# Windowed attention in front of two expert layers: scores issued one unit earlier on four PSUM banks, and half of the probability copies on ScalarE

## The chip, the cores and the metric

One core of a Trainium2 chip runs the whole program. The metric is the device time of one execution in microseconds (us); lower is better. Three timed runs of the kernel before took 779.24, 786.21 and 785.84 us, so the median is 785.84 us. One more execution was taken with the hardware profiler, and every row below is from that one.

## What is computed

```python
def reference(**kwargs):
    ...
    attn_out = _attn_ref(**attn_kwargs)          # B=4, H=8, 512 local + 32 global tokens, head size 64
    x = attn_out.transpose(0, 2, 1, 3).reshape(B * S, H * D)   # 2176 x 512
    x = _moe_ref(x=x, **moe_kwargs)              # top-1 of 8 experts, 512 -> 1024 -> 512, ReLU
    return _moe2_ref(x=x, **moe2_kwargs)         # 512 -> 2048 -> 512 with a piecewise square
```

The attention is the part that the change touches. A local query sees the 32 global keys and the local keys at most 32 positions away; a global query sees all 544 keys. Both go through a softmax over their keys.

```python
    s_g = scale * np.matmul(q_g, k_all.transpose(0, 1, 3, 2))
    out_g = np.matmul(sm(s_g), v_all)
    mask = np.abs(pos[:, None] - pos[None, :]) <= 32
    s_ll = np.where(mask, scale * np.matmul(q_l, k_l.transpose(0, 1, 3, 2)), -1e9)
    s_l = np.concatenate([scale * np.matmul(q_l, k_g.transpose(0, 1, 3, 2)), s_ll], axis=-1)
    out_l = np.matmul(sm(s_l), np.concatenate([v_g, v_l], axis=2))
```

## The kernel before

The attention works on the 32 (batch, head) pairs in order. Heads 2c and 2c+1 form a *pair* c: their queries and keys share one SBUF tile (64 partitions each), and there are 16 pairs. The work is cut into *units*: 32 units "h" (one local head each) and 8 units "g" (the global queries of four heads). The list `units` (L538 to L544) has a g unit ahead of every four h units, with two exceptions (the first and the last g unit).

The parts that one head goes through are separate functions, and the loop at L577 calls them in different units, so that each part finds its input ready:

- `s_pair(c)` (L209): for both heads of a pair, one matmul each with a mask matrix (L213) opens a PSUM bank and adds 0 or -1e30, then 32 small matmuls (L218) add the scores. It runs in the even unit, the one of head 2c.
- `s_max(n)` (L221): VectorE takes the row maxima out of PSUM (L225) and negates them (L226). Then it does up to 8 small operations of a list `fill` (routing of earlier tokens to experts).
- `s_exp(n)` (L232): ScalarE takes the exponentials, four instructions of 128x128 with a running sum (L239).
- `t_head(n)` (L287), two units later: TensorE transposes the four 128x128 blocks into a PSUM bank (L294), VectorE copies the bank to the SBUF tile `pto` (L295).
- `pv(c)` (L328), one unit after the second head's `t_head`: 64 small matmuls with the values (L339), then VectorE multiplies by the reciprocal sum (L342 to L344) into `xr`.
- `x_turn(b, g)` (L351), one unit later through the list `tasks`: TensorE transposes `xr`, ScalarE copies the result to `xT` (L355). After four pairs (one batch) `logits`, `logits_t` and the list of `route` follow.
- The g units do the same with `s_glob` (L242), `g_max`, `g_exp` (L267), `t_glob` (L299, six transposes into two banks, copied by ScalarE at L306), `pv_glob` (L310).

The order of the instructions on each of TensorE, VectorE, ScalarE and the SyncE DMA queue is exactly the order in which the code issues them (the schedule is manual for these four), and each engine works through its own list in order. What an instruction waits for is set by the tiles. PSUM has 8 banks: before, 3 for the tag "s" (the scores of two heads and of a global unit share them), 3 for the tag "to" (every transpose target), one for "x" (the output of `pv`), and one, `gxb`, for small things. A new tile of a tag takes a bank whose last user has to be done.

The loads of keys, queries and values are issued by SyncE (`load_k`, `load_q`, `load_v`) into 4, 3 and 3 buffers, in the odd units after the tasks, or behind `pv`. GpSimd spreads the values (`spread_v`). After the attention come the tail of the routing, the expert layer and the last layer (from about 155 us on), which the change doesn't touch except for line numbers.

Of the kernel before, what the change touches and what calls it, by code (L numbers as in the profile page):

```python
# [35 lines left out]
NB = 24  # L36
# [75 lines left out]
def emit(tc, d, out):  # L112
# [51 lines left out]
    nc.vector.memset(warm, 0.0)  # L164
    wps = ps.tile([128, 512], F32, tag="s", name="sp", bufs=3)
    for _ in range(9):
# [42 lines left out]
    def s_pair(c):  # L209
        k, q = ks[c], qp[c]  # L210
        for z in range(2):
            sps[2 * c + z] = ps.tile([128, 4, BW], F32, tag="s", name="sp", bufs=3)
            nc.tensor.matmul(sps[2 * c + z].rearrange("p i w -> p (i w)"), lhsT=mask[:, 0:128], rhs=mask[:, 128:], start=True, stop=False)  # L213
        for j in range(NG):
            i, a = divmod(j, 4)
            for z in range(2):
                r = slice(64 * z, 64 * z + 64)
                nc.tensor.matmul(sps[2 * c + z][a * WIN:(a + 1) * WIN, i, :], lhsT=q[r, j * WIN:(j + 1) * WIN],  # L218
                                 rhs=k_at(k, r, j), start=False, stop=(i == 3))
# [22 lines left out]
    def s_glob(q):  # L242
        sp = ps.tile([128, 512], F32, tag="s", name="sp", bufs=3)
        for part in range(3):
            for j in range(4):
                c, z = 2 * q + j // 2, 64 * (j % 2)
                k = ks[c][z:z + 64].rearrange("p (n w) -> p n w", w=WIN)
                p = slice(j * SG, (j + 1) * SG)
                o, r = ((sp[p, 0:320], ks[c][z:z + 64, 0:320]),
                        (sp[p, 320:480], k[:, 15:24:2, :]), (gxb[p, 0:64], k[:, 10:13:2, :]))[part]  # L250
                nc.tensor.matmul(o, lhsT=qg[z:z + 64, c, :], rhs=r, start=True, stop=True)
        gsp[q] = sp
# [34 lines left out]
    def t_head(n):  # L287
        c, z = divmod(n, 2)
        if z == 0:
            pt[c] = ap.tile([128, 2, 512], F32, tag="pto", name="pto", bufs=3)  # L290
        p = pexp.pop(n)
        o = ps.tile([128, 4, 128], F32, tag="to", name="ps_o", bufs=3)
        for i in range(4):
            nc.tensor.transpose(o[:, i, :], p[:, i, :], ident)  # L294
        nc.vector.tensor_copy(pt[c][:, z, :], o.rearrange("p i q -> p (i q)"))  # L295

    pgt, grec = {}, {}

    def t_glob(q):  # L299
        pg = gexp.pop(q)  # L300
        pgt[q] = ap.tile([128, 6, 128], F32, tag="pgt", name="pgt", bufs=2)
        for m0, m1 in ((0, 4), (4, 6)):
            o = ps.tile([128, 4, 128], F32, tag="to", name="ps_o", bufs=3)
            for m in range(m0, m1):
                nc.tensor.transpose(o[:, m - m0, :], pg[:, m * 128:(m + 1) * 128], ident)
            nc.scalar.activation(pgt[q][:, m0:m1, :], o[:, 0:m1 - m0, :], AF.Copy)  # L306
# [21 lines left out]
    def pv(c):  # L328
        b, g = divmod(c, 4)
        p, v = pt.pop(c), vt[c]  # L330
        if g == 0:
            xr[b] = ap.tile([128, 4, DM], F32, tag="xr", name="xr", bufs=2)
            xT[b] = ap.tile([128, 4, SL], F32, tag="xT", name="xT", bufs=2)
        xo = ps.tile([128, 4, 2, D], F32, tag="s" if c == 15 else "x", name="xo", bufs=3 if c == 15 else 1)
        for i in range(4):
# [15 lines left out]
    def x_turn(b, c):  # L351
        o = ps.tile([128, 4, 128], F32, tag="to", name="ps_x", bufs=3)
        for i in range(4):
# [4 lines left out]
    def logits(b):  # L358
        o = ps.tile([128, 512], F32, tag="to", name="lg", bufs=3)
        for c in range(4):  # L360
# [6 lines left out]
    def logits_t(b):  # L367
        o = ps.tile([128, 4, 4, 32], F32, tag="to", name="lg", bufs=3)
        for i in range(4):
# [3 lines left out]
    def logits3():  # L373
        o = ps.tile([128, 512], F32, tag="to", name="lg", bufs=3)
        for c in range(3):
# [5 lines left out]
    def part3():  # L381
        o = ps.tile([128, 4, 4, 32], F32, tag="to", name="lg", bufs=3)
        for i in range(4):
# [11 lines left out]
    def glob_turn():  # L395
        o = ps.tile([128, 4, 128], F32, tag="to", name="ps_x", bufs=3)
        for c in range(4):
# [96 lines left out]
    def zlist():  # L494
        o = ps.tile([128, 512], F32, tag="to", name="ip", bufs=3)[:, 0:1]
        for t in range(NE):
# [8 lines left out]
    def zsteps():  # L505
        o = ps.tile([128, 4, 128], F32, tag="to", name="ps_x", bufs=3)
        for k in range(4):
# [3 lines left out]
        for g in range(2):  # L511
            o = ps.tile([128, 4, 128], F32, tag="s", name="zh", bufs=3)
            for u in range(4):
# [58 lines left out]
    for c in range(3):  # L572
        spread_v(c)
    pend_n, pend_g, pend_v = [], [], []
    LT, LG = 2, 3
    nv = 3
    for s in range(len(units)):  # L577
# [5 lines left out]
        if gq[0] == "g":  # L583
            t_glob(gq[1])
            pend_g.append(gq[1])
        if kind == "h":
            if a % 2 == 0:
                s_pair(a // 2)
        elif kind == "g":
            s_glob(a)  # L590
        while tasks:
            if tasks.pop(0)() == 1:
                break
        if kind == "h" and a % 2 == 1:
            if a // 2 + 4 < 16:
# [122 lines left out]
    zz(24)  # L718
    ip = ps.tile([128, 512], F32, tag="to", name="ip", bufs=3)[:, 0:NB]
    for t in range(NT):  # L720
# [525 lines left out]
```

## Time and profile before

| | |
|---|---|
| timed runs | 779.24, 786.21, 785.84 us, median 785.84 us |
| the profiled execution's own time | 777.55 us |
| its span, first to last instruction | 775.8 us |
| share of the span: TensorE, VectorE, ScalarE busy | 96%, 67%, 46% |
| mean granted TensorE clock | 0.991 |

The profiled execution took 777.55 us with 1.75 us outside its span, and lies 8.29 us under the median of the timed runs. Times in the rows are in us from the start of the span. A timeline row gives start, duration, engine, line, operation, output and inputs, shapes and a count, and in brackets how long the engine was idle before it and who released it. "PE" is TensorE's matmul side and "PEld" its weight loads; DVE is VectorE, ACT ScalarE, POOL GpSimd, SPq SyncE's queue of DMA issues. Consecutive instructions of one kind are merged into one row, so a row that took long for its count has waits inside.

### The profile page before, as it was taken

The numbers are of one execution on the slowest core, as the hardware profiler recorded it, in microseconds if no ns is written. First come the engines' busy times: TensorE is split into PE (matmuls) and PEld (weight loads), VectorE is DVE, ScalarE is ACT, GpSimd is POOL, SyncE is SP. The second block draws the span as 40 slices with busy tenths as digits, with TensorE's granted clock in tenths as the row PEclk, the third lists the DMA queues.
The fourth block names the chain that finished last, engine by engine and source line by source line (L and its number), as shares of the span: only waits on it lengthen the run. The fifth ranks groups of instructions, "written<-read, shape, count | busy, mean of one in ns | idle before, by whom it ended". The sixth has DMA issues, their size and how long they took to land.

```text
span 775.8 us, 16281 instructions
## 1 busy us (share of the span) xinstructions
PE 742.9 (96%) x6525; PEld 645.5 (83%) x6539; DVE 520.8 (67%) x988; ACT 360.6 (46%) x775; POOL 123.9 (16%) x164
## 2 busy tenths in 40 slices
PE   7898868899999999999999999999999999999996
PEld 3666646699899899899899989999898999999994
DVE  3687856758956956957477767767875787555443
ACT  3667545355755855854345554323432442322221
POOL 2536423231122122111100000000000000002112
PEclk9999999999999999999999999999999999999999
DMA  8868872188968956912142221110220100001111
GB/s 259 260 195 254 269 236 76 39 295 316 347 201 274 351 197 242 361 47 82 61 124 82 71 93 54 55 55 1 66 88 11 55 1 0 1 1 68 54 41 68
DMA packets 41954, 103.77 MB, mean 134 GB/s; under 512 B 6798, under 2 KB 11278, under 8 KB 39824
## 3 DMA queue, kind: packets, MB, share of 16 engines
q1 hardware_dynamic: 37312, 88.48, 34.3%
q0 software_dynamic: 4560, 14.19, 4.9%
q8 instruction: 53, 0.87, 0.5%
q14 instruction: 29, 0.24, 0.1%
HBM read 93.45 MB, written 14.18 MB: 139 GB/s over the span
## 4 chain that ended last, share of the span: by engine, by line
PE 72%; issue 6%; POOL 1%; DVE 1%; ACT 0%; POOLq 0%
PE fh L919 7%; PE fh L920 7%; PE fh L921 7%; PE o L920 7%; PE o L921 7%; PE o L919 7%; PE hp L919 5%; PE hp L921 5%; PE hp L920 5%; PE yp L921 5%; PE yp L919 4%; PE yp L920 4%; PE xTp L902 1%; POOL out_dram L1160 1%; PE yTp L813 1%
## 5 line engine op out<-in xcount | busy, mean ns | idle before, releaser
L1107 DVE SCALAR_TENSOR_TENSOR r<-r 128x384 f32<-128x384 f32 (+1 forms) x96 | 51.4, 535 | 120.0 <-ACT r L1106 119.8
L1106 ACT ACTIVATE r<-fh,half 128x384 f32<-128x384 f32 (+1 forms) x96 | 54.0, 563 | 115.1 <-PE fh L921 114.9
L921 PE MATMUL o<-wh,gl 128*128 128x512 f32 x272 | 107.5, 395 | 0.0
L919 PE MATMUL o<-wh,gh 128*128 128x512 f32 x272 | 107.4, 395 | 0.0
L920 PE MATMUL o<-wl,gh 128*128 128x512 f32 x272 | 107.3, 394 | 0.0
L1109 ACT ACTIVATE gh<-g 128x384 fp32r<-128x384 f32 (+1 forms) x96 | 48.8, 508 | 125.5 <-DVE g L1108 125.5
L920 PE MATMUL fh<-yl,wh 128*128 128x384 f32 (+1 forms) x320 | 104.4, 326 | 0.0
L919 PE MATMUL fh<-yh,wh 128*128 128x384 f32 (+1 forms) x320 | 104.3, 326 | 0.0
L921 PE MATMUL fh<-yh,wl 128*128 128x384 f32 (+1 forms) x320 | 104.2, 326 | 0.0
L1160 POOL DMA_INDIRECT out_dram<-acc,rid x17 | 16.5, 969 | 368.3 <-DVE acc L1158 366.8
L919 PE MATMUL hp<-xTh,w1h 128*128 128x256 f32 x256 | 72.5, 283 | 1.8 <-PEq L1051 1.8
L921 PE MATMUL hp<-xTh,w1l 128*128 128x256 f32 x256 | 72.5, 283 | 0.0
L920 PE MATMUL hp<-xTl,w1h 128*128 128x256 f32 x256 | 72.5, 283 | 0.0
L920 PEld LDWEIGHTS fh<-yl,wh 128*128 128x128 f32 x320 | 60.1, 188 | 3.6 <-DVE rid L817 0.2
L919 PEld LDWEIGHTS fh<-yh,wh 128*128 128x128 f32 x320 | 60.1, 188 | 3.5
L921 PEld LDWEIGHTS o<-wh,gl 128*128 128x128 f32 x272 | 51.1, 188 | 12.4 <-DVE gl L1115 0.8
L919 PE MATMUL yp<-w2h,hTh 128*128 128x512 f32 x152 | 60.4, 398 | 0.0
L921 PEld LDWEIGHTS fh<-yh,wl 128*128 128x128 f32 x320 | 60.1, 188 | 0.0
L921 PE MATMUL yp<-w2h,hTl 128*128 128x512 f32 x152 | 59.6, 392 | 0.0
L920 PE MATMUL yp<-w2l,hTh 128*128 128x512 f32 x152 | 59.3, 390 | 0.0
L920 PEld LDWEIGHTS o<-wl,gh 128*128 128x128 f32 x272 | 51.1, 188 | 7.9
L919 PEld LDWEIGHTS o<-wh,gh 128*128 128x128 f32 x272 | 51.1, 188 | 7.8
(232 smaller groups left out, 1573.8 us busy)
## 6 DMA issues: line engine op xcount, KB each, us to landing
w1r<-in_w SPq DMA_DIRECT2D x44, 512.0 KB, 5.7
w2r<-in_w SPq DMA_DIRECT2D x44, 512.0 KB, 5.3
wraw<-in_wf SPq DMA_DIRECT2D x16, 1024.0 KB, 4.9
ks<-in_k SPq DMA_DIRECT2D x16, 400.0 KB, 5.5
v<-in_v SPq DMA_DIRECT2D x16, 384.0 KB, 3.8
yr<-ys SPq DMA_DIRECT2D x17, 256.5 KB, 2.7
qp<-in_q SPq DMA_DIRECT2D x16, 256.0 KB, 6.5
xs<-xr SPq DMA_DIRECT2D x8, 512.0 KB
```

The lines of the kernel that those rows point to most:

```text
L813: nc.tensor.transpose(p[:, k, :], a[:, k * 128:(k + 1) * 128], ident)
L902: nc.tensor.transpose(p[:, k, :], src[:, k * 128:(k + 1) * 128], ident)
L919: nc.tensor.matmul(o, lhsT=ah, rhs=bh, start=first, stop=False)
L920: nc.tensor.matmul(o, lhsT=ah, rhs=bl, start=False, stop=False)
L921: nc.tensor.matmul(o, lhsT=al, rhs=bh, start=False, stop=last)
L1106: nc.scalar.activation(r[:, 0:w], o[:, 0:w], AF.Relu, bias=half, scale=0.5)
L1107: nc.vector.scalar_tensor_tensor(r[:, 0:w], r[:, 0:w], 1.0, r[:, 0:w], ALU.min, ALU.mult)
L1109: nc.scalar.activation(gh[:, 0:w], g[:, 0:w], AF.Copy)
L1160: w = nc.gpsimd.indirect_dma_start(out=out, out_offset=bass.IndirectOffsetOnAxis(ap=rid[:, tt:tt + 1].bitcast(U32), axis=0), in_=a, in_off ...
```

## The change

PSUM: the tag "s" gets 4 banks, the tag "to" 2. `s_pair(0)` is issued ahead of the loop. In the loop `s_pair(c + 1)` is issued in the odd unit of pair c, after the tasks and ahead of the loads, instead of `s_pair(c)` in the even unit of its own pair. `t_head` of every odd head has its bank copied by ScalarE instead of VectorE.

```diff
-        o = ps.tile([128, 4, 128], F32, tag="to", name="ps_o", bufs=3)
+        o = ps.tile([128, 4, 128], F32, tag="to", name="ps_o", bufs=2)
         for i in range(4):
             nc.tensor.transpose(o[:, i, :], p[:, i, :], ident)
-        nc.vector.tensor_copy(pt[c][:, z, :], o.rearrange("p i q -> p (i q)"))
+        if z:
+            nc.scalar.activation(pt[c][:, z, :], o.rearrange("p i q -> p (i q)"), AF.Copy)
+        else:
+            nc.vector.tensor_copy(pt[c][:, z, :], o.rearrange("p i q -> p (i q)"))
...
+    s_pair(0)
     pend_n, pend_g, pend_v = [], [], []
...
-        if kind == "h":
-            if a % 2 == 0:
-                s_pair(a // 2)
-        elif kind == "g":
+        if kind == "g":
             s_glob(a)
         while tasks:
             if tasks.pop(0)() == 1:
                 break
+        if kind == "h" and a % 2 == 1 and a < 31:
+            s_pair(a // 2 + 1)
         if kind == "h" and a % 2 == 1:
             if a // 2 + 4 < 16:
                 load_k(a // 2 + 4)
```

Every other `bufs=3` of the tags "s" and "to" becomes 4 and 2 in the same way (`wps`, `s_pair`, `s_glob`, `t_glob`, the last `pv`, `x_turn`, `logits`, `zlist`, `zsteps` and the other users).

On TensorE, in the middle of the attention (the g unit of the 6th group of four heads, then its first three h units), this stands in the kernel before; L294 is `t_head`, L213 and L218 `s_pair`, L354 `x_turn`, L339 `pv`, L305 `t_glob`:

```order
L339 MATMUL xo<-v,pto 32x64 x32
L294 MATMUL ps_o<-ident,p 128x128 x4
L213 LDWEIGHTS mask
L213 MATMUL sp<-mask 128x512
L213 LDWEIGHTS mask
L213 MATMUL sp<-mask 128x512
L218 MATMUL sp<-ks,qp 32x128 x32
L354 MATMUL ps_x<-ident,xr 128x128 x4
L339 MATMUL xo<-v,pto 32x64 x32
L294 MATMUL ps_o<-ident,p 128x128 x4
L305 MATMUL ps_o<-ident,pgz_121 128x128 x6
```

and this in the changed kernel, whose line numbers are 3 higher from `pv_glob`, `pv` and `x_turn` on (L342 is `pv`, L357 `x_turn`, L308 `t_glob`):

```order
L342 MATMUL xo<-v,pto 32x64 x32
L294 MATMUL ps_o<-ident,p 128x128 x4
L357 MATMUL ps_x<-ident,xr 128x128 x4
L213 LDWEIGHTS mask
L213 MATMUL sp<-mask 128x512
L213 LDWEIGHTS mask
L213 MATMUL sp<-mask 128x512
L218 MATMUL sp<-ks,qp 32x128 x32
L342 MATMUL xo<-v,pto 32x64 x32
L294 MATMUL ps_o<-ident,p 128x128 x4
L308 MATMUL ps_o<-ident,pgz_121 128x128 x6
```

The scores have moved behind `x_turn`, which now follows one `t_head` after the `pv` that feeds it, and they belong to the next pair. `t_glob` is followed by `x_turn` and not by scores.

On ScalarE, from the global exponentials (L275) of the next group on, before; L239 is `s_exp`, L355 the copy of `x_turn`, L306 those of `t_glob`:

```order
L275 ACTIVATE pgz_120,sg<-sp,m_2059 128x5x64
L275 ACTIVATE pgz_120,sg<-sp,m_2059 128x5x32
L275 ACTIVATE pgz_120,sg<-gxb,m_2059 128x2x32
L355 ACTIVATE xT<-ps_x 128x512
L239 ACTIVATE p,ss<-sp,mn 128x128 x8
L306 ACTIVATE pgt<-ps_o 128x512
L306 ACTIVATE pgt<-ps_o 128x256
```

and in the changed kernel, where L296 is the new copy of an odd head, L358 that of `x_turn`, L309 those of `t_glob`:

```order
L275 ACTIVATE pgz_120,sg<-sp,m_2095 128x5x64
L275 ACTIVATE pgz_120,sg<-sp,m_2095 128x5x32
L275 ACTIVATE pgz_120,sg<-gxb,m_2095 128x2x32
L296 ACTIVATE pto<-ps_o 128x512
L358 ACTIVATE xT<-ps_x 128x512
L239 ACTIVATE p,ss<-sp,mn 128x128 x8
L309 ACTIVATE pgt<-ps_o 128x512
```

A copy of an odd head now stands between the global exponentials and the copy of `x_turn`.

On VectorE, from the `t_head` of the first head of a group to the next g unit, before (L295 are the copies, L225 and L226 `s_max`, L318 the global output):

```order
L295 COPY pto_1555<-ps_o_1556 128x512
L225 TENSOR_REDUCE mx4_1616<-sp_1573 128x4
L226 TENSOR_SCALAR mn_1617<-mx4_1616 128x4
L295 COPY pto_1555<-ps_o_1625 128x512
L225 TENSOR_REDUCE mx4_1642<-sp_1575 128x4
L226 TENSOR_SCALAR mn_1643<-mx4_1642 128x4
L318 TENSOR_SCALAR xgo_1670<-gxb_119,rg_1488 128x64
L295 COPY pto_1682<-ps_o_1683 128x512
```

and in the changed kernel (L298 are the copies that stay, L321 the global output):

```order
L298 COPY pto_1591<-ps_o_1592 128x512
L225 TENSOR_REDUCE mx4_1616<-sp_1498 128x4
L226 TENSOR_SCALAR mn_1617<-mx4_1616 128x4
L225 TENSOR_REDUCE mx4_1678<-sp_1500 128x4
L226 TENSOR_SCALAR mn_1679<-mx4_1678 128x4
L321 TENSOR_SCALAR xgo_1706<-gxb_119,rg_1488 128x64
L298 COPY pto_1718<-ps_o_1719 128x512
```

The copy of the odd head is gone from the middle; the rest stands as before. SyncE's list of DMA issues is the same in both kernels.

## Rows read from the trace of the kernel before

**Rows 1.** Stretch, length, busy PE, PEld, DVE, ACT, POOL (count), PEclk, DMA share, GB/s

```profile
65.20:79.90 14.70, 13.73 (x373) 9.87 (x374) 10.39 (x26) 10.16 (x49) 8.08 (x17) 1.00 0.80 249
79.90:94.30 14.40, 12.52 (x365) 8.86 (x367) 12.74 (x41) 8.48 (x40) 6.08 (x8) 1.00 0.84 263
112.60:131.30 18.70, 13.73 (x362) 10.92 (x362) 15.09 (x54) 9.86 (x46) 9.22 (x15) 0.91 0.32 90
155.00:775.80 620.80, 612.03 (x3424) 551.97 (x3424) 416.07 (x670) 276.27 (x419) 62.02 (x54) 1.00 0.34 118
```

**Rows 2.** Timeline of TensorE, 69 to 92 us

```profile
69.45 1.38 PE L294 MATMUL ps_o<-ident,p 128*128 128x128 f32 x4
...
78.15 1.10 PE L339 MATMUL xo<-v,pto 128*32 128x64 f32 x64
79.18 0.66 PE L294 MATMUL ps_o<-ident,p 128*128 128x128 f32 x4
79.89 0.38 PE L213 MATMUL sp<-mask 128*128 128x512 bf16 x1
...
81.28 0.66 PE L354 MATMUL ps_x<-ident,xr 128*128 128x128 f32 x4
...
83.59 1.37 PE L294 MATMUL ps_o<-ident,p 128*128 128x128 f32 x4 [0.62 <-ACT p L239]
84.80 0.82 PE L305 MATMUL ps_o<-ident,pgz 128*128 128x128 f32 x6
...
88.42 0.66 PE L354 MATMUL ps_x<-ident,xr 128*128 128x128 f32 x4 [1.06 <-DVE pto L295]
...
90.25 1.24 PE L294 MATMUL ps_o<-ident,p 128*128 128x128 f32 x4
```

**Rows 3.** Timeline of TensorE: rows that resume inside a group

```profile
37.83 0.64 PE L218 MATMUL sp<-ks,qp 64*32 64x128 f32 x23 [1.76 <-issue]
...
67.42 0.41 PE L218 MATMUL sp<-ks,qp 64*32 64x128 f32 x3 [0.80 <-issue]
...
99.57 1.71 PE L339 MATMUL xo<-v,pto 128*32 128x64 f32 x52 [2.86 <-issue]
```

**Rows 4.** Timeline of ScalarE, 78 to 85 us

```profile
78.72 0.53 ACT L275 ACTIVATE pgz<-sp,m 128x320 f32<-128x320 f32 x1 [1.22 <-DVE ri L342]
...
81.98 0.60 ACT L355 ACTIVATE xT<-ps_x 128x512 f32<-128x512 f32 x1 [1.97 <-PE ps_x L354]
...
83.10 0.35 ACT L239 ACTIVATE p<-sp,mn 128x128 f32<-128x128 f32 x1
...
84.12 0.37 ACT L239 ACTIVATE p<-sp,mn 128x128 f32<-128x128 f32 x1
```

**Rows 5.** Timeline of VectorE, 79 to 88 us

```profile
79.32 0.69 DVE L344 TENSOR_TENSOR xr<-xo,ri 128x512 f32<-128x512 f32 x1 [0.38 <-PE xo L339]
...
81.39 0.69 DVE L225 TENSOR_REDUCE mx<-sp 128x4 f32<-128x512 f32 x1 [0.79 <-PE sp L218]
...
82.20 0.28 DVE L416 TENSOR_REDUCE L<-lg 128x32 f32<-128x128 f32 x1
...
85.15 0.20 DVE L281 TENSOR_SCALAR rg<-sg 128x1 f32<-128x1 f32 x1
...
87.68 0.68 DVE L295 COPY pto<-ps_o 128x512 f32<-128x512 f32 x1
```

**Rows 6.** Groups of instructions, 20 to 100 us: busy us, mean ns

```profile
L295 DVE COPY pto<-ps_o 128x512 f32<-128x512 f32 x21 | 14.4, 684 | 1.3 <-PE ps_o L294 1.1
...
L355 ACT ACTIVATE xT<-ps_x 128x512 f32<-128x512 f32 x11 | 6.6, 597 | 15.2 <-PE ps_x L354 15.2
```

**Rows 7.** Timeline near the start: a query load's issue and TensorE

```profile
19.25 0.35 SPq L179 DMA_DIRECT2D qp<-in_q  x1
...
22.46 0.38 PE L213 MATMUL sp<-mask 128*128 128x512 bf16 x1
```

**Rows 8.** DMA issues up to 30 us: KB each, us to landing

```profile
qp<-in_q SPq DMA_DIRECT2D x6, 256.0 KB, 7.6
```

**Rows 9.** The last stretch of the attention on TensorE

```profile
116.94 1.12 PE L354 MATMUL ps_x<-ident,xr 128*128 128x128 f32 x4 [2.85 <-DVE xr L344]
```

More of the change, by code (lines that the diff above doesn't have):

```diff
@@ L164, in emit @@
     nc.vector.memset(warm, 0.0)
-    wps = ps.tile([128, 512], F32, tag="s", name="sp", bufs=3)
+    wps = ps.tile([128, 512], F32, tag="s", name="sp", bufs=4)
     for _ in range(9):
@@ L211, in s_pair @@
         for z in range(2):
-            sps[2 * c + z] = ps.tile([128, 4, BW], F32, tag="s", name="sp", bufs=3)
+            sps[2 * c + z] = ps.tile([128, 4, BW], F32, tag="s", name="sp", bufs=4)
             nc.tensor.matmul(sps[2 * c + z].rearrange("p i w -> p (i w)"), lhsT=mask[:, 0:128], rhs=mask[:, 128:], start=True, stop=False)
@@ L242, in s_glob @@
     def s_glob(q):
-        sp = ps.tile([128, 512], F32, tag="s", name="sp", bufs=3)
+        sp = ps.tile([128, 512], F32, tag="s", name="sp", bufs=4)
         for part in range(3):
@@ L302, in t_glob @@
         for m0, m1 in ((0, 4), (4, 6)):
-            o = ps.tile([128, 4, 128], F32, tag="to", name="ps_o", bufs=3)
+            o = ps.tile([128, 4, 128], F32, tag="to", name="ps_o", bufs=2)
             for m in range(m0, m1):
@@ L333, in pv @@
             xT[b] = ap.tile([128, 4, SL], F32, tag="xT", name="xT", bufs=2)
-        xo = ps.tile([128, 4, 2, D], F32, tag="s" if c == 15 else "x", name="xo", bufs=3 if c == 15 else 1)
+        xo = ps.tile([128, 4, 2, D], F32, tag="s" if c == 15 else "x", name="xo", bufs=4 if c == 15 else 1)
         for i in range(4):
@@ L351, in x_turn @@
     def x_turn(b, c):
-        o = ps.tile([128, 4, 128], F32, tag="to", name="ps_x", bufs=3)
+        o = ps.tile([128, 4, 128], F32, tag="to", name="ps_x", bufs=2)
         for i in range(4):
@@ L358, in logits @@
     def logits(b):
-        o = ps.tile([128, 512], F32, tag="to", name="lg", bufs=3)
+        o = ps.tile([128, 512], F32, tag="to", name="lg", bufs=2)
         for c in range(4):
@@ L367, in logits_t @@
     def logits_t(b):
-        o = ps.tile([128, 4, 4, 32], F32, tag="to", name="lg", bufs=3)
+        o = ps.tile([128, 4, 4, 32], F32, tag="to", name="lg", bufs=2)
         for i in range(4):
@@ L373, in logits3 @@
     def logits3():
-        o = ps.tile([128, 512], F32, tag="to", name="lg", bufs=3)
+        o = ps.tile([128, 512], F32, tag="to", name="lg", bufs=2)
         for c in range(3):
@@ L381, in part3 @@
     def part3():
-        o = ps.tile([128, 4, 4, 32], F32, tag="to", name="lg", bufs=3)
+        o = ps.tile([128, 4, 4, 32], F32, tag="to", name="lg", bufs=2)
         for i in range(4):
@@ L395, in glob_turn @@
     def glob_turn():
-        o = ps.tile([128, 4, 128], F32, tag="to", name="ps_x", bufs=3)
+        o = ps.tile([128, 4, 128], F32, tag="to", name="ps_x", bufs=2)
         for c in range(4):
@@ L494, in zlist @@
     def zlist():
-        o = ps.tile([128, 512], F32, tag="to", name="ip", bufs=3)[:, 0:1]
+        o = ps.tile([128, 512], F32, tag="to", name="ip", bufs=2)[:, 0:1]
         for t in range(NE):
@@ L505, in zsteps @@
     def zsteps():
-        o = ps.tile([128, 4, 128], F32, tag="to", name="ps_x", bufs=3)
+        o = ps.tile([128, 4, 128], F32, tag="to", name="ps_x", bufs=2)
         for k in range(4):
@@ L511, in zsteps @@
         for g in range(2):
-            o = ps.tile([128, 4, 128], F32, tag="s", name="zh", bufs=3)
+            o = ps.tile([128, 4, 128], F32, tag="s", name="zh", bufs=4)
             for u in range(4):
@@ L718, in emit @@
     zz(24)
-    ip = ps.tile([128, 512], F32, tag="to", name="ip", bufs=3)[:, 0:NB]
+    ip = ps.tile([128, 512], F32, tag="to", name="ip", bufs=2)[:, 0:NB]
     for t in range(NT):
```

## The prediction

> **What bounds the kernel now.** I read the busy time by stretch first. From 155 us on TensorE is busy 612.03 of 620.80 us [rows 1], and the change touches nothing there, so it can only act on the attention, the first 131 us or so. One batch of the attention takes two stretches of about 14.5 us, one for each group of four heads. In the first shown TensorE is busy 13.73 of 14.70 us, in the second 12.52 of 14.40; VectorE 10.39 and 12.74, ScalarE 10.16 and 8.48 [rows 1]. No engine is full by itself, VectorE comes closest in the second stretch, and TensorE sets the pace as long as the others feed it.
>
> Then TensorE's timeline, for its stalls. Four transposes of a head take 0.66 us where nothing holds them (79.18), but 1.38, 1.37 and 1.24 us at 69.45, 83.59 and 90.25, where each waits for one of the four exponentials, and at 83.59 TensorE was idle 0.62 us before [rows 2]. That is the stall the change aims at: 0.72 us in the first stretch, and 0.62 + 0.71 + 0.58 = 1.91 us in the second. A fourth one, 1.06 us at 88.42, waits for VectorE's copy of an earlier head [rows 2]: together 2.97 us in the second stretch. The cause shows on ScalarE: it stood 1.97 us idle until the transposes of `x_turn` came at 81.98, and the exponentials behind them in its list began only at 83.10 [rows 4]; VectorE had waited 0.79 us for the scores at 81.39 [rows 5].
>
> A third kind of gap is no wait of the program: TensorE stopped in the middle of a group for 1.76, 0.80 and 2.86 us, with nothing that released it [rows 3]. I read it as late instruction supply. The Trainium skill ("Runtime: NRT & Kernel Launch", "Instruction fetch mechanics") says that crossing an instruction page is mostly hidden; these rows, 5.42 us in all, show it open. By the page the gaps would be nothing to reckon with; by the rows they are noise that the change doesn't aim at, and I leave them as they are.
>
> **The change part by part.** *Scores one unit earlier.* Nothing is added: the same matmuls, mask and scores, from 79.89 to 81.28, so 1.39 us a pair [rows 2], stand elsewhere. The maximum, and behind it the exponential, no longer waits for them, so the stalls at the head transposes should go: -0.72 in the first stretch, -1.91 in the second, and the 1.06 us goes too, since `x_turn` no longer waits on that copy, though the copy itself is as late as ever (next part). I credit 2.97 and 0.72. Four banks make it possible: the bank of the second head of `s_pair` in the first odd unit of a group was last used by the global scores, so it waits for the second of the global exponentials, not for the head just begun. These start at 78.72 [rows 4] and read that bank for about 0.9 us, to 79.6, before TensorE could be there: no wait.
>
> *What the scores had covered.* `x_turn` now comes one `t_head` after `pv`. VectorE's product `xr` began at 79.32, right after `pv` (78.15 + 1.10 = 79.25), and took 0.69, to 80.01 [rows 2, 5]; TensorE would want it at 79.18 + 0.6 = 79.8. In the second stretch the transposes of `x_turn` also share a bank with the `t_head` just ahead, as the other of the two is held by the routing's logits; that bank is emptied by ScalarE, behind the global exponentials, which end near 79.9, and a copy of 0.60 [rows 4, 6] puts it at 80.5. New stall: 0.5 us in the first stretch, 0.75 in the second.
>
> *Two banks for transposes.* The second part of `t_glob` takes the bank of the `t_head` ahead of it, and so waits for VectorE's copy. In the second stretch that copy ended at 87.68 + 0.68 = 88.36, which is 9.04 us after `xr` began [rows 5]. Taken off: the copy of the odd head, 0.6 of the 0.684 us of rows 6 (the rest overlapped), and the 0.79 us wait. That leaves 7.65. TensorE gets there from the end of `pv` in 0.6 (transposes) + 0.65 (stall of above, beyond the transposes) + 0.55 (`x_turn`) + 1.39 (scores) + 1.05 (`pv`) + 0.6 + 0.55 = 5.4. New stall: 2.2 us. In the first stretch the routing block on VectorE from 82.20 to 85.15 [rows 5], 2.95 us, is missing; 7.65 - 2.95 = 4.7 is earlier than 5.2, and only the copy's own 0.68 beside half a group of transposes shows: 0.2 us. The Trainium skill ("Perfetto Trace Analysis", "Matmuls") says that independent groups should rotate through different PSUM banks so that the emptying of one overlaps the matmuls of the next. It speaks against this part, and with three banks the same place (84.80) went through without a wait [rows 2]. By it the two banks cost what I reckon or more; that is the rival on the slow side below.
>
> *Odd heads copied by ScalarE.* 16 copies of 0.684 us leave VectorE, 16 of about 0.597 come to ScalarE [rows 6], two in each stretch. ScalarE was idle 4.5 and 5.9 us of a stretch [rows 1]; they hide there except where counted above. Behind such a copy in ScalarE's list stand the exponentials of the next head, 84.12 + 0.37 - 83.10 = 1.39 us [rows 4], which are used two units later.
>
> *Loads.* Queries are wanted one unit earlier. A load issued at 19.25 with 7.6 us to landing [rows 7, 8] is there at 26.9 at the latest; TensorE did `s_pair(2)` at 22.46 [rows 7], and would stand ahead of `s_pair(3)` at about that time now, with the scores of pair 2 already done. Bounds: a gain of 1.5 us (it lands at 23, and the early stalls go), a loss of 2 (it lands at 27, and everything behind waits). I take +0.3, near the middle. Later, a load is issued more than a stretch ahead.
>
> *The last batch.* From 112.60 on VectorE is busy 15.09 of 18.70 us [rows 1], and TensorE waited 2.85 us for its `xr` at 116.94 [rows 9]. Four copies fewer take 2.4 us off VectorE there; other waits stand in line, so between 0 and -2.4; I take -1.2.
>
> **The sum.** First stretch: -0.72 + 0.5 + 0.2 = 0.0. Second: -2.97 + 0.75 + 2.2 = 0.0. To these I add that VectorE, with 1.2 us less to do in a stretch, catches up a little: -0.3 us a batch, three batches, -0.9 (bounds -4 and +3, from 0 to all of what is counted as new stall being half or one and a half times as large). With +0.3 and -1.2 that is -1.8 us: 777.55 - 1.8 = 775.75 us for the profiled execution. The median of the runs lies 8.29 us higher, and against it the same difference gives 785.84 - 1.8 = 784.0 us.
>
> **Rivals.** *Slower: two banks are too few.* Place: the second part of `t_glob` and the `x_turn` transposes. If VectorE or ScalarE is further behind than in this trace (each waits for TensorE in its own list, and a stall of one is passed on), each of the new stalls grows. I count 3.65 us of them a batch; they would have to reach 3.65 + 1.8/3 = 4.25 to make the change worth nothing, and another 2.6 us a batch to cost over 1%. Twice as large in all three batches gives 784.0 + 11 = 795 us. For it: 2.2 us is from one row; against it: the scores come so early that VectorE no longer waits for them.
>
> *Faster: the new stalls don't come.* If VectorE, relieved of the odd copies and of its waits for scores, runs ahead of TensorE, the copy is done in time, and all old stalls are gained: 3.69 us a batch, three batches, and 2.4 at the end: -13 us, 773 us. For it: VectorE has 4.3 us idle in the first stretch; against it: 1.7 in the second [rows 1].
>
> *No effect: supply.* The DMA engines are busy 0.80 and 0.84 of the time in these stretches [rows 1], at 249 and 263 GB/s, and TensorE stood still without a releaser three times [rows 3]. What is gained waits for keys, values or instructions: 786 us, plus or minus 2.
>
> *It doesn't do what it says.* If the second bank of `s_pair` had been that of the head just begun, its scores would wait for that head's exponentials (78.72 + 1.2 + 1.2 + 1.39 = 82.5 instead of 80.5), 2 us a stretch, +13 us, 799. The program assigns it the bank of the global scores, so I give this 0.02.
>
> **How the numbers follow.** About 1%, 7.8 us, is what a measurement of this kernel can tell from no change. The forecast (784.0) has 0.50, supply 0.20, both within 1%; faster 0.20, of which 0.18 passes 1%; slower 0.10 with the misread bank, all over 1%. That is 0.18 faster, 0.72 within, 0.10 slower. The range has to take in the faster case, 773, and the lower half of the slower one: 772 to 792.
>
> **What would show it.** Right: transposes of a head at 0.66 us nearly everywhere, no idle time of VectorE before the maxima, a stall of TensorE before the second part of `t_glob` (about 2 us in every second stretch) and one of 0.5 to 0.75 before `x_turn`, stretches of 14 to 14.5 us. Wrong: stretches of 13 us or less (the faster rival), or over 15 (the slower one); a wait for scores at the mask matmul of the second head; a wait for a query load after the start.

## The result: 5.7 us slower, and the profile after

Sixteen runs of each kernel: 789.40 us median after, 784.27 us before (its first three had given 785.84). The ratio of the two is 1.0073, 95% interval 1.0045 to 1.0100, so the change costs 0.73% of 784.27, 5.7 us, where I had forecast a gain of 1.8. Three of the sixteen runs after stood in a slower state (793.67 to 794.38 us, granted clock 0.976 to 0.978); without them the means are 788.32 and 783.80 us, 4.5 us apart, so the loss is 4 to 6 us and what is reckoned from 1.0073 below can be about 1 us too large. The profiled execution of the changed kernel took 786.55 us, its span is 784.8 us (775.8 before), and its mean granted clock is 0.984 (0.991). These two executions differ by 9.00 us, more than the medians do: that of the kernel before lies 6.7 us below its median, that of the changed kernel 2.9 us. What follows reads the difference of the two profiles, so it is larger than the loss in the median.

I cut the attention at the global scores of a group (L251), which stand in both kernels, and at the last `ranks`. Busy time by stretch, before: one batch in two stretches, then from the 7th to the 8th group's global scores, then all that is left of the attention, which I call the last batch (columns as in [rows 1]).

```profile
61.65:76.51 14.86, 13.35 (x370) 9.36 (x371) 11.07 (x30) 9.90 (x46) 10.50 (x18) 1.00 0.89 272
76.51:91.41 14.90, 13.01 (x370) 9.37 (x371) 12.59 (x38) 8.75 (x41) 4.10 (x9) 1.00 0.79 246
91.41:107.61 16.20, 11.49 (x309) 8.90 (x311) 8.88 (x26) 7.42 (x34) 7.53 (x13) 0.89 1.01 332
107.61:138.43 30.82, 25.68 (x630) 20.20 (x632) 20.42 (x68) 15.92 (x67) 10.65 (x19) 0.94 0.29 84
```

The same four stretches after:

```profile
63.84:78.75 14.91, 12.87 (x370) 8.85 (x371) 8.35 (x23) 11.15 (x49) 9.09 (x16) 1.00 0.76 238
78.75:93.57 14.82, 12.15 (x370) 9.23 (x371) 11.24 (x41) 9.70 (x43) 6.09 (x12) 1.00 0.83 272
93.57:110.20 16.63, 10.06 (x244) 7.43 (x244) 7.16 (x20) 7.32 (x32) 6.11 (x11) 0.84 0.98 322
110.20:147.18 36.98, 28.78 (x629) 21.88 (x631) 17.78 (x64) 17.68 (x70) 10.64 (x19) 0.84 0.22 61
```

A batch takes as long as before (29.73 and 29.76 us), with TensorE less busy in it (25.02 against 26.36). The last batch is 6.16 us longer, and its granted clock has fallen from 0.94 to 0.84. TensorE's timeline in the second stretch answers [rows 2]:

```profile
81.42 0.66 PE L294 MATMUL ps_o<-ident,p 128*128 128x128 f32 x4
82.80 0.66 PE L357 MATMUL ps_x<-ident,xr 128*128 128x128 f32 x4 [0.72 <-ACT pto L296]
83.50 0.38 PE L213 MATMUL sp<-mask 128*128 128x512 bf16 x1
...
87.44 0.31 PE L342 MATMUL xo<-v,pto 128*32 128x64 f32 x6 [1.47 <-issue]
87.69 0.66 PE L294 MATMUL ps_o<-ident,p 128*128 128x128 f32 x4
...
89.16 0.44 PE L308 MATMUL ps_o<-ident,pgz 128*128 128x128 f32 x2 [0.38 <-DVE pto L298]
```

The head transposes take 0.66 us, the old stalls are gone, and `x_turn` waits 0.72 us for ScalarE's copy (forecast 0.75). But the second part of `t_glob` waits 0.38 us and not 2.2, and in front of it stands a gap that I hadn't reckoned with there: 1.47 us of "issue", that is, TensorE stood still and the profile shows nothing that it waited for. I call such gaps *stops*. More rows of that kind, which answer [rows 3]:

```profile
36.28 0.53 PE L342 MATMUL xo<-v,pto 128*32 128x64 f32 x20 [2.14 <-issue]
57.47 0.58 PE L342 MATMUL xo<-v,pto 128*32 128x64 f32 x25 [1.41 <-issue]
66.95 0.24 PE L342 MATMUL xo<-v,pto 128*32 128x64 f32 x1 [0.96 <-issue]
100.00 1.09 PE L218 MATMUL sp<-ks,qp 64*32 64x128 f32 x57 [1.59 <-issue]
106.93 1.11 PE L308 MATMUL ps_o<-ident,pgz 128*128 128x128 f32 x4 [4.00 <-issue]
```

With the 1.47 and one of 0.21 (at 71.26) that is 11.78 us from the third to the last group's global scores. Before it was the 5.42 us of [rows 3] and one more, which the profile puts down to VectorE (the instruction named had ended at 105.84, 0.75 us earlier, so I count it as a stop):

```profile
106.59 0.66 PE L354 MATMUL ps_x<-ident,xr 128*128 128x128 f32 x4 [1.75 <-DVE mn L226]
```

together 7.17 us. The growth doesn't hang on this one pair of executions: in the profiles of `p_copy` and `before_warm` below, which have the same TensorE list there as the kernel before, these stops sum to 7.8 and 7.3 us, in those of `p_score` and `after_warm`, with the list of the changed kernel, to 11.0 and 10.1.

The last batch, answering [rows 9]:

```profile
120.31 0.66 PE L357 MATMUL ps_x<-ident,xr 128*128 128x128 f32 x4 [2.96 <-DVE xr L347]
...
123.53 0.69 PE L308 MATMUL ps_o<-ident,pgz 128*128 128x128 f32 x2 [1.09 <-ACT pto L296]
...
131.74 0.63 PE L294 MATMUL ps_o<-ident,p 128*128 128x128 f32 x4 [0.67 <-DVE zidx L501]
...
138.51 0.63 PE L511 MATMUL ps_x<-ident,xgb 128*128 128x128 f32 x4 [2.26 <-DMA xgb<-xs,zidx]
```

And the stretches of low granted clock after (column PEclk, 0.50 is 1.2 GHz of 2.4):

```profile
36.70:40.11 3.41, 3.19 (x40) 2.33 (x42) 2.98 (x10) 1.96 (x7) 0.79 (x2) 0.50 0.54 166
104.97:111.79 6.82, 4.60 (x28) 3.06 (x32) 0.00 (x0) 3.21 (x12) 2.08 (x3) 0.50 0.64 210
122.03:128.86 6.83, 5.50 (x110) 3.76 (x112) 2.02 (x10) 3.71 (x17) 4.73 (x7) 0.50 0.05 3
139.10:142.51 3.41, 3.41 (x73) 3.24 (x73) 0.69 (x1) 1.02 (x2) 0.00 (x0) 0.50 0.00 0
```

Each begins in or soon after an idle stretch of TensorE of 2 to 4 us: the stops of 2.14 and 4.00 us, the waits of 2.96 and 2.26. The reverse doesn't always hold: a stop of 2.69 us at 35.96 in `after_raw8` and a wait of 2.88 us at 111.23 in `before_noload` have no fall of the clock in or behind them. Before, the only stretch of low clock between the third and the last group's global scores is

```profile
99.47:102.88 3.41, 3.31 (x60) 3.14 (x61) 1.21 (x2) 0.35 (x3) 0.00 (x0) 0.50 1.04 303
```

What low clock costs can be read from the timed runs of the changed kernel: at a mean clock of 0.989 one took 781.87 us, at 0.976 another 792.12; 2 x 0.013 x 788 = 20.5 us more at 1.2 GHz, 10.25 us more time, half of it. A straight line through all sixteen gives 0.49 us for each us at the low level.

### The profile page after: what moved, and what is told of

It is laid out like the page before. It is cut to its first block, busy times and chain, and to the rows that moved or that the text cites. A ratio compares the mean times of both kernels' runs of the same rounds, so it can differ in the third digit from the quotient of the medians.

```text
span 784.8 us, 16278 instructions
## 1 busy us (share of the span) xinstructions
PE 742.8 (95%) x6524; PEld 645.1 (82%) x6539; DVE 507.4 (65%) x972; ACT 368.4 (47%) x791; POOL 126.3 (16%) x164
## 4 chain that ended last, share of the span: by engine, by line
PE 68%; issue 6%; DVE 1%; POOL 1%; DMA 1%; ACT 1%; POOLq 0%; SPq 0%; ACTq 0%; DVEq 0%
PE fh L922 7%; PE fh L923 7%; PE fh L924 7%; PE o L923 7%; PE o L924 7%; PE o L922 7%; PE hp L922 4%; PE hp L924 4%; PE hp L923 4%; PE yp L924 4%; PE yp L922 4%; PE yp L923 4%; POOL out_dram L1163 1%; PE xTp L905 1%; DMA w1r<-in_w 1%
```

## What the stops are

The stops stand at certain places of TensorE's list. Between 66.95 and 71.26 it has 126 + 128 records, between 87.44 and 100.00 250 + 253, before between 37.83 and 67.42 757 + 761: multiples of 253 or so, and with the 1 or 2% of records that are missing, of 256 (matmuls and weight loads together). I call such a block of 256 instructions a *page* and its end a *boundary*. The trace has a queue q8 of kind "instruction": 53 packets, 0.87 MB in all in the kernel before, about one for each page of TensorE's 13064 records. After the boundary at 100.00 (the view is from 98.5 on) the DMA view shows none on q8 until 104.37, and then one (columns: packets, MB, share of 16 engines):

```profile
q1 hardware_dynamic: 981, 2.01, 104.1%
q14 instruction: 1, 0.01, 0.5%
...
q1 hardware_dynamic: 443, 0.90, 100.1%
q8 instruction: 1, 0.02, 2.8%
```

The data queue q1 fills the engines at both times. In both kernels each of the stops counted above ends 1.4 to 1.6 us after such a packet has landed. So I read them thus: as TensorE crosses a boundary, the next page is asked for; its packet queues behind data, and TensorE stops if it has run through its page before that packet is there. (When a packet is asked for, the trace doesn't show; only when it starts. That it queues is my reading, which the runs below test.) The Trainium skill ("Runtime: NRT & Kernel Launch", "Instruction fetch mechanics") has the same blocks of 256 instructions and calls the cost of crossing from one to the next mostly hidden. The size agrees with the counts here; the second doesn't hold here, where one boundary cost 4.00 us.

The decisive rows are those from boundary to boundary while the raw weights of the expert layer load, before and after:

```profile
99.57:106.59 7.02, 5.21 (x128) 4.39 (x129) 2.32 (x4) 1.12 (x4) 2.24 (x3) 0.76 1.05 327
```

```profile
100.00:106.93 6.93, 2.93 (x127) 2.40 (x126) 2.06 (x4) 1.06 (x7) 2.02 (x3) 0.86 1.04 336
```

The page takes 7 us in both. Before, TensorE needed 5.27 of them for its content (`pv`, transposes, scores, partly at the low clock: 0.76 in the row) and stood 1.75; after, the page holds scores and `pv` with one `t_head`, is done in 2.93, and TensorE stands 4.00 us in one piece. What was gained became idle time, and the low clock from 104.97 came on top. My theory then was *supply*: late pages cost the time. The rival was *waits*: the two banks and ScalarE's copies cost it.

## Experiments

Ratios are to the kernel before on the same chip, with 95% intervals.

**Without the loads.**

```diff
     def load_k(c):
+        if c > 3:
+            ks[c] = ks[c - 4]
+            return
```

and the same for queries and values, from pair 3 on. The kernel leaves these loads out and works on the tiles of earlier pairs, so it computes something else.

> The kernel before, with the loads of keys, queries and values left out from the fourth, third and third pair on (later pairs reuse the tiles of the first ones, so their results are not those of the reference); the stores and the eight raw weight loads stay. Supply theory (TensorE stops at a boundary of 256 of its instructions when the 16 KB packet that holds the next 256 is late because it queues behind data): packets start under 1 us after the boundary instead of 1.7 us on average, the stops at 18.17, 37.83 and 67.42 (0.49, 1.76, 0.80 us) go, those of 2.86 and 1.75 us near 100 shrink to half; 784.3 - 5 = about 779 us. Rival, the stops have nothing to do with data transfers: 784 us, the same stops.

> The changed kernel with the same loads left out (results not those of the reference). Supply theory: about 12 us of stops and what they cost in granted clock were the loss, so they go here: 789.4 - 11 = about 778 us, equal to or 1 to 3 us below the kernel before with the same loads left out. Rival, two banks and the copies on ScalarE cost the time through waits of the program: it stays 4 to 6 us above the kernel before with the same loads left out.

The total times (819.53 before, 816.66 us after, where I had expected 779 and 778) say nothing, as other rows go to the experts; the stretches of the attention do. Before, one batch and the last one:

```profile
60.27:88.07 27.80, 26.14 (x742) 18.67 (x741) 23.12 (x68) 18.86 (x86) 14.00 (x25) 1.00 0.35 100
101.88:134.35 32.47, 26.17 (x631) 20.16 (x631) 19.89 (x68) 15.95 (x67) 8.43 (x16) 0.95 0.17 52
```

After:

```profile
59.32:87.17 27.85, 24.59 (x742) 17.73 (x741) 20.00 (x63) 20.67 (x92) 13.97 (x26) 1.00 0.41 122
97.42:128.04 30.62, 24.39 (x631) 18.76 (x631) 16.48 (x64) 17.89 (x71) 8.41 (x16) 1.00 0.20 58
```

Between the third and the last group's global scores the stops fall from 7.17 to 2.28 us before and from 11.78 to 1.15 after, and a batch takes the same in both kernels, 2 us less than with loads. The last batch is 1.85 us shorter after the change (1.6 of it is clock). So the order of the work by itself doesn't cost 5 us. The packets show what the data do to them: behind the boundaries at 95.76 (before) and 92.52 (after) q1 takes 9.1% and 9.8% of the engines, and q8's packet starts 1.09 and 1.13 us after the boundary (I had expected under 1), against 4.38 us at 100.00 above, where q1 takes 104.1%. The waits that I had forecast come out here, where no stop covers them:

```profile
76.92 0.66 PE L366 MATMUL ps_x<-ident,xr 128*128 128x128 f32 x4 [0.71 <-ACT pto L305]
...
82.76 0.44 PE L317 MATMUL ps_o<-ident,pgz 128*128 128x128 f32 x2 [0.98 <-DVE pto L307]
```

**Raw weight loads later.** In both kernels, with 10 and then with 8 in place of 16:

```diff
-        if s >= len(units) - 16 and raw:
+        if s >= len(units) - 10 and raw:
```

> The kernel before with the eight raw weight loads issued 6 units later (the last 10 units instead of the last 16). Supply theory: the two stops near 100 us (2.86 and 1.75 us) fall to under 0.5 us each, the stretch of low clock behind them goes, and a smaller stop may come near 115 to 125; 784.3 - 4 = about 780 us. Rival, these loads don't matter: 784 us.

> The changed kernel with the same later issue. Supply theory: the stops of 1.59 and 4.00 us near 100 to 107 go and with them the low clock from 105 to 112; 789.4 - 7 = about 782 us, so that the two kernels differ by 2 us or less. Rival, the last batch is longer because of its own waits (x_turn, second part of t_glob, gather): it stays 5 us or more above the kernel before with the same later issue.

> The changed kernel with the raw weight loads in the last 8 units (16 in the changed kernel, 10 in the run with later loads). Supply theory: as with 10 or up to 2 us less, since the loads then fall wholly behind those of keys, queries and values: 0.5 to 0.8% below the kernel before, and no stop over 2 us from 95 to 112 us. If the other place was only lucky, it lies at or above the kernel before again.

> The kernel before with the same place. Supply theory: 0.2 to 0.5% below the kernel before, so the changed kernel in this place is 0 to 4 us faster.

| loads in the last | before | after |
|---|---|---|
| 16 units | 1 | 1.0073 (1.0045 to 1.0100) |
| 10 units | 0.9973 (0.9946 to 1.0000), 779.14 us | 0.9947 (0.9915 to 0.9978), 777.73 us |
| 8 units | 0.9921 (0.9894 to 0.9948), 776.00 us | 0.9953 (0.9927 to 0.9979), 778.01 us |

The changed kernel gains 9.9 and 9.4 us (1.0073 less 0.9947 and 0.9953, of 784), the kernel before 2.1 and 6.2. For the kernel before I had expected a little more in the first place (4 us) and less in the second (2 to 4 us). With later loads neither kernel is reliably the faster: the changed one is 0.26% below the other in the one place, 0.32% above it in the other, where I had expected it 0 to 4 us faster. The page that took 6.93 us takes 5.24 now (changed kernel, 10 units):

```profile
96.44:101.68 5.24, 2.95 (x136) 2.42 (x135) 3.67 (x12) 3.12 (x17) 3.23 (x8) 1.00 0.86 269
```

Its stop is 2.29 us and not gone, as I had expected, and others came at 121 to 124 us (2.06 after, 2.60 before), as the loads now stand there. With 8 units the changed kernel's stop there is 0.52 us, and one of 2.89 us comes at 123.75. All four versions of the table's last two rows lie below both kernels, the kernel before with 10 units only just, and the fastest is the kernel before with the loads in the last 8 units.

**The parts alone.** `p_copy` is the kernel before with only the ScalarE copies; `p_score` is the changed kernel with all copies on VectorE again:

```diff
-        if z:
-            nc.scalar.activation(pt[c][:, z, :], o.rearrange("p i q -> p (i q)"), AF.Copy)
-        else:
-            nc.vector.tensor_copy(pt[c][:, z, :], o.rearrange("p i q -> p (i q)"))
+        nc.vector.tensor_copy(pt[c][:, z, :], o.rearrange("p i q -> p (i q)"))
```

> The kernel before with only the copies of odd heads on ScalarE (three and three banks, scores where they were). Supply theory: TensorE's list is that of the kernel before, instruction for instruction, so the boundaries stand at the same places and the time is that of the kernel before within 2 us (781 to 785). Rival, ScalarE's list is where the time is lost: 3 to 5 us above the kernel before.

> The changed kernel with all copies on VectorE again (four and two banks, early scores). Supply theory: TensorE's list is that of the changed kernel, so the dense page near 100 us meets the raw weight loads as there, a stop of about 4 us follows, and the time is 4 to 7 us above the kernel before. Rival, the copies on ScalarE make the loss: equal to the kernel before.

`p_copy`: 0.9987 (0.9955 to 1.0019), 782.18 us. `p_score`: 1.0057 (1.0025 to 1.0089), 785.67 us. In the old order the copies cost nothing that shows; the early scores with their split of the banks make the loss. Which of these two does it stays open: no run has four and two banks with the scores in their old place. The page near 100 us is there again in `p_score`, in the same 6.93 us with the same stop of 4.00:

```profile
99.39:106.32 6.93, 2.93 (x127) 2.51 (x128) 2.77 (x8) 2.08 (x12) 2.23 (x3) 1.00 1.05 346
```

**The boundaries moved.** More or fewer warm-up matmuls, 2 instructions each, move every boundary through the program; the work and its order stay.

```diff
-    for _ in range(9):
+    for _ in range(5):
         nc.tensor.matmul(wps, lhsT=warm[:, 0:128], rhs=warm, start=True, stop=True)
+    for _ in range(100):
+        nc.tensor.matmul(wps[0:32, 0:64], lhsT=warm[:, 0:32], rhs=warm[:, 0:64], start=True, stop=True)
```

> The changed kernel with 192 more TensorE instructions at its start (the 9 warm-up matmuls become 5 wide and 100 of 64 columns), so that every boundary of 256 instructions falls 192 instructions earlier in the program. Supply theory: the stops come at the new boundaries and not at the old places; with 4.6 us of queueing near 91 to 103 and 2.0 elsewhere, the pages of this position run 3.0 and 4.5 us there, which gives stops of 4.1 and 2.6 us, 13.9 us of stops in all and four of over 2 us, 5.8 us more than with 224. So about 790 to 793 us. Rival, the place of the boundaries is of no matter and the loss is in the order of the work: the same as the changed kernel, 789 us.

> The same with 224 more instructions (116 matmuls of 64 columns). Supply theory: pages of 5.2 and 6.3 us near 91 to 103, stops of 1.9 and 0.8 us there, 10.9 us in all and one of over 2 us, so 5 to 8 us less than with 192 and 2 to 3 us less than the changed kernel: about 785 to 787 us. Rival: equal to the run with 192 within 1 us, and to the changed kernel.

> The changed kernel with one warm-up matmul instead of nine, so 16 TensorE instructions fewer at the start and every boundary of 256 falls 16 instructions later in the program. Supply theory: the page that begins near 100 us then runs 5.3 us instead of 2.7 (it takes in two groups of transposes and their waits), so its stop falls from 4.0 to about 1.8 us and the stretch of low clock behind it goes: 3 to 5 us below the changed kernel, apart from what the shorter warm-up costs at the start (to be read at the third group's global scores, 32.22 us in the changed kernel; at most 2 us). Rival, the place of the boundaries is of no matter: as the changed kernel, plus that cost.

> The changed kernel with 8 more warm-up matmuls of 64 columns, so every boundary falls 16 instructions earlier; they add about 0.3 us at the start. Supply theory: the page near 98 to 100 us runs 2.3 us, the shortest there is, and its stop stays at 4 to 5 us: the time of the changed kernel or 1 to 2 us more, and 3 to 6 us above the run with 16 fewer. Rival: no difference between the two beyond the start.

The first pair missed: 1.0057 (1.0029 to 1.0085) with 192, 1.0084 (1.0049 to 1.0119) with 224, so 192 is not the slower one; I had expected it to be slower by 5 to 8 us. The stops did come at the new places, but not in the sizes that one queueing time for all pages gave: 3.02 us at 46.48 with 192, where I had reckoned less. I had also forgotten that 100 matmuls take time: the third group's global scores start at 36.18 us in place of 32.22. Without these 4 us (0.5%) the two lie 0.1 and 0.3% above the kernel before, less than the changed kernel by about the width of the intervals. From the third group's global scores on the stops sum to 7.7 us with 192, near those of the kernel before, though the work and its order are those of the changed kernel. With 224 they sum to 6.0 us, and yet the time is a little higher, so the sum of the stops in one profile doesn't order these two. My sum over the boundaries was too coarse to say how much their place is worth. The second pair: 1.0092 (1.0058 to 1.0125) with 16 fewer, 1.0141 (1.0104 to 1.0178) with 16 more, 0.49% or 3.8 us apart, within the 3 to 6 us expected, though the two intervals overlap a little. The start doesn't explain it: with 16 fewer the third group's global scores begin at 33.81 us, with 16 more at 31.57, so the slower one has the earlier start by 2.24 us. In the profile with 16 more,

```profile
109.48 0.37 PE L344 MATMUL xo<-v,pto 128*32 128x64 f32 x2 [4.74 <-issue]
```

and with 16 fewer the stop falls to 0.57 us, and the next page pays:

```profile
104.96 0.94 PE L218 MATMUL sp<-ks,qp 64*32 64x128 f32 x49 [0.57 <-issue]
...
111.80 0.65 PE L294 MATMUL ps_o<-ident,p 128*128 128x128 f32 x4 [2.50 <-ACT p L239]
```

The profile puts the last row down to an exponential; the last of these ended at 111.24, so a part of the 2.50 us is a wait of the program. From boundary to boundary this is 6.84 us, and 7.23 (102.25 to 109.48) with 16 more: again about 7 us, though the pages hold 4.3 and 2.5 us of work and waits. Against the changed kernel itself the shorter warm-up won nothing, where I had expected 3 to 5 us: that part missed.

**TensorE kept busy in two waits of the last batch.**

```diff
     def x_turn(b, c):
         o = ps.tile([128, 4, 128], F32, tag="to", name="ps_x", bufs=2)
+        if (b, c) == (B - 1, 0):
+            busy(o, 12)
```

and `busy(o, 8)` at the head of `zsteps`, in both kernels; `busy` multiplies the warm-up tile with itself into the bank that the transposes behind overwrite.

> The changed kernel with 12 useless matmuls of 512 columns in the wait of the last batch's first x_turn (2.96 us) and 8 in the wait for the gathered rows (2.26 us), each into the PSUM bank that the transposes behind them overwrite. Clock theory: no idle stretch is left there, so the stretches of low clock at 122.0 (6.8 us) and 139.1 (3.4 us) go, and with them half their length: 5 us less than the changed kernel, so within 1 us of 0.1% above the kernel before. Rival, waits and order: no change, 0.7% above the kernel before.

> The kernel before with the same matmuls in the same two waits (2.85 and 1.80 us). Clock theory: the stretch of low clock at 116.5 (3.4 us) goes, 1.7 us less than the kernel before. Rival: no change, or 0.5 us more for the matmuls that outlast the waits.

> The changed kernel with later raw weight loads and the same matmuls. Clock theory: its low clock at 121.4 stands behind a stop of 2.06 us at a boundary, which the matmuls don't fill, so 0 to 2 us less than without them: 0.5 to 0.8% below the kernel before.

> The kernel before with later raw weight loads and the same matmuls. Clock theory: its low clock at 123.4 stands behind a stop of 2.60 us, so 0 to 1 us less than without them: 0.3% below the kernel before.

The changed kernel: 1.0032 (1.0005 to 1.0059), 783.55 us. The kernel before: 1.0013 (0.9994 to 1.0032), where I had expected 1.7 us less; its profile has no low clock from 108.33 us to the end of the attention, but the last batch takes 30.24 us for 30.82, so here little came back. With later loads 0.9979 (0.9960 to 0.9997) for the changed kernel, less of a gain than the 0.5 to 0.8% expected, and 0.9980 (0.9954 to 1.0007) for the kernel before, near the 0.3% expected. Of the changed kernel's last batch the profile now says

```profile
108.05:141.74 33.69, 30.16 (x648) 20.89 (x651) 17.53 (x64) 17.71 (x70) 10.68 (x19) 0.95 0.25 73
```

33.69 us at a clock of 0.95, in place of 36.98 at 0.84. The stop ahead of it is still there, with the low clock behind it:

```profile
104.78 1.11 PE L308 MATMUL ps_o<-ident,pgz 128*128 128x128 f32 x4 [4.02 <-issue]
```

Useless work in place of idle time took off 3.2 us (0.41%; I had expected 5). I read that share of the loss as clock and not order; the intervals of the two ratios overlap, and in the kernel before the same work won nothing. At nearly the clock of the kernel before, the last batch is still 2.9 us longer than its 30.82.

**Scores ahead of the tasks.**

```diff
+        if kind == "h" and a % 2 == 1 and a < 31:
+            s_pair(a // 2 + 1)
         while tasks:
             if tasks.pop(0)() == 1:
                 break
-        if kind == "h" and a % 2 == 1 and a < 31:
-            s_pair(a // 2 + 1)
```

> The changed kernel with the early scores ahead of the tasks, so that x_turn comes behind the scores instead of ahead of them and stands between the scores and the next pv. The waits of x_turn (0.5 to 0.7 us in each stretch, for xr or for ScalarE's copy) go, and no page holds scores and pv side by side without transposes between. Supply theory: the waits' time goes into stops, the stop near 105 us stays at 2 us or more because the raw weight loads still queue there: 784 to 788 us. Rival, the waits of the program are the loss: the time of the kernel before or 2 us below it.

> The same order with the raw weight loads 6 units later. Supply theory: at or up to 2 us below the changed kernel with later raw weight loads alone (777.7), so 775 to 778 us, the fastest of all. Rival, waits of the program are the loss: 3 to 4 us below it (4 times 0.5 and 3 times 0.7 us).

The edit didn't do what I meant: most `x_turn` are issued one unit earlier than these scores, and only `logits`, `logits_t` and a few more moved; the wait of 0.69 us for ScalarE's copy is still there. So the two are nearly repeats of earlier runs: 1.0053 (1.0018 to 1.0087), and with the loads in the last 10 units 0.9993 (0.9966 to 1.0020), again 0.6% between the two places of the raw weight loads. The second is 780.11 us, where I had expected the fastest of all (775 to 778), and lies 0.46% above the changed kernel with the same loads. My idea about `x_turn` stays untried.

## Why the prediction was wrong

Point by point, by its own steps.

*Old stalls, new stalls.* Right in place, and in size but for one term. Head transposes at 0.66 us, `x_turn` 0.72 (0.75 forecast) and 0.20 to 0.67 (0.5), the first stretch's second part of `t_glob` 0.37 (0.2). The 2.2 us of the second stretch is 0.38 with loads (I take it that VectorE catches up during the stop ahead of it; that isn't shown) and 0.98 and 1.61 without: mis-sized by a half. The sum of "0.0 and 0.0 us a stretch" comes out without the loads, 27.80 and 27.85 us a batch. With them, 29.76 and 29.73, it comes out by luck: the batch holds 2.64 us of stops after the change and 0.80 before, so the order had won 1.9 us, which the stops took.

*Odd copies on ScalarE hide.* Right as far as the time of `p_copy` shows.

*Loads at the start, +0.3.* The size was near, the place not: `s_pair(3)` went through without a wait, the scores of the second pair waited 2.23 us for their queries at 9.98. The third group's global scores start at 32.22 (32.09 before): +0.13.

*The gaps: "I leave them as they are".* This is the step that failed. They are not noise: their places are fixed by the list, their length by how much of the time until the next page is there TensorE uses up, and the change shortens just that. They grew from 7.17 to 11.78 us, a term that the prediction put at nothing. The rival "supply" had the mechanism, but as a ceiling (no gain), and left out that a long stop can bring low clock with it. That 789.4 us still lies inside the range of 772 to 792 is luck: its upper part was there for the two banks, whose waits came out smaller than forecast.

*No term for the clock.* From the third to the last group's global scores the profiled executions differ by 77.98 - 75.52 = 2.46 us. The stops are +4.6. Of low clock there are 8.64 us in place of 3.41; 1.96 us of it lie inside the stop of 4.00 us and 0.10 inside that of 2.86, where they cost nothing more, and the rest, 6.68 in place of 3.31, is +1.7 at one half. What is left, -3.8, is by this account what the change did win, and gave back. In the last batch, +6.16, the clock is at most (1 - 0.84) x 36.98 - (1 - 0.94) x 30.82 = 5.9 - 1.8 = +4.1 us (some of it falls into waits), and the waits of 1.09 (ScalarE's copy of an odd head, two banks), 0.67 and the longer ones for `xr` and the gather (0.11 and 0.46) are +2.3.

*The last batch, -1.2.* It is -1.85 us without loads, nearly all of it clock; with them the sign is wrong, +6.16, most of it the clock and the rest waits, as above. The 2.85 us wait for `xr`, from which I wanted to win, is still 2.96.

What stays open: these accounts are of one execution each, and the size of a single stop varies from run to run, so I can't divide the 5.7 us to better than a microsecond or two. The timed runs give one estimate of the clock's share: averaged over the runs, the granted clock is 0.981 in the changed kernel and 0.986 to 0.988 in the repeats of the kernel before that were run beside the experiments. That is 7 to 11 us more at the low level, and at one half or a little less some 3 to 5 us of time. Shown are three things: the loss comes with the raw weight loads in their old place and goes with the loads later, the early scores with their split of the banks bring it and not the copies, and the stops grow with the changed list. That the stops and the low clock are the whole of it is argued from single profiles. What the split of the banks does by itself is not known.

## What to carry to other kernels

A gap of "issue" in the middle of a group is a term like any other: see whether it stands at equal distances in the engine's list, and what the data queues do then. Where pages of instructions come late, taking waits out of a page wins nothing, and packing it denser gathers the same idle time into one long stop; moving the data off that stretch paid here (2 to 10 us, by one number). Spreading the data out was not tried. Idle stretches of TensorE, of 2 to 4 us here, can be paid twice, the second time as 3.4 or 6.8 us at half the clock.

## What I had not expected of the hardware

While the 4 MB of raw weights loaded, the page of 256 TensorE instructions that began near 100 us took 6.1 to 7.7 us in the nine profiles with these loads in their old place where both its ends show, with 2.5 to 5.6 us of it for its own work and waits, and the rest a stop. And of five places of the boundaries (the changed kernel and the four that moved them) none was without a stop of 2 us or more somewhere in the attention.
